# Fused block-sparse attention and gated feed-forward on one core: another TensorE order inside a loop step

## Chip, cores, metric

The kernel runs on one core of one Trainium2 chip. The metric is the device time of one execution in microseconds (us), taken as the median of several runs. Differences are told in us and in per cent of that median.

## What is computed

```python
# attention: 4 batches, 8 heads, 768 positions, 64 per head; blocks of 32
scores = q @ k.T / sqrt(64)                  # kept where the block mask allows
# mask: own block and its neighbours, first and last block row and column,
#       and 3 sampled blocks per block row
attn = softmax(scores);  x = attn @ v        # then tokens x 512
# feed-forward: 3072 tokens, 512 -> 2048 -> 512
h = x @ w_in
out = (h * erf(softplus(h))) @ w_out
```

All of it is done in one launch, from inputs in DRAM to the output in DRAM.

## The kernel before, in words

**Attention units.** Each batch has 15 units, 60 in all: 11 "m" units, each with two block rows and their eight key blocks, and 4 "f" units, which are the dense first and last block rows. A unit passes through `scores` (L619: f32 products on TensorE into `s_m` or `s_f`, one PSUM buffer, `ps_s`, for all units), `soft_max` (L563: the maximum, DVE), `soft_exp` (L572: exponentials `pf` and the high half `p2` in f16, ACT), `soft_low` (L608: the low half on DVE, then a transposing DMA from SP's queue into `pT`). Three unit steps later (`PV_LAG`) follow `values` (L646: `pT` times the gathered values, into `po`), `norm` (L683: the division, DVE, into `xf`, one buffer) and `turn` (L708: a cast on ACT and a subtraction on DVE split `xf` into halves `x2`, and a transposing DMA from SP's queue puts them into `xT`). An m unit gives one such place; of the f units every second one does.

**Feed-forward groups.** Every four places make a chunk, 12 chunks in all; each has 8 groups of 256 hidden columns. A group passes through `ff_first` (L735: 24 matmuls `h<-xT,wi`; three PSUM buffers), `ff_logs` (L759: five activations on ACT), `ff_power` (L772, DVE), `ff_exp` (L777, ACT), and two groups later (`GATE_LAG`) `ff_gate` (L781, DVE, the last reader of `h`) and `ff_halves` (L786, DVE, writes `g`); three groups later (`FF_LAG`) `ff_second` (L794: 12 matmuls `o<-wo,g`), and at a chunk's last group `ff_store` (L807).

**The loop.** L982 runs over 96 groups and three more steps. A step takes one group, and, where the table `spread` says so, one unit and the values of the unit three before: four to seven of a chunk's eight steps have attention work. A step that has both a unit and values is called a full step below; there are 45 of them with a step number of 3 or more, 7 with a unit and no values, 2 with values and no unit. From step 3 on the engines keep the order in which the step is written (`held`, L984); before that, and in the prologue, a scheduler orders the instructions, the loads and the decoding of the weights among them. On TensorE a full step is written: values, first product, scores, second product.

**Values of the next batch.** `behind` (L858) loads, measures and splits the next batch's values in pieces of one unit step each: `load_v` puts the load of `vraw` (one buffer) into SP's queue, and one unit step later `max_v` (L226) reduces it on DVE. SP's queue is in order: each of its DMAs waits for its own data, and all behind it wait too.

```python
if place: values(*place); used_values(place)
if group: ff_first(*group); ff_logs(*group)
if steps: gathers()
if unit:  scores(unit); used_keys(unit)
if m >= FF_LAG: ff_second ...; ff_store ...
```

Of the kernel before, what the change touches and what calls it, by code (L numbers as in the profile page):

```python
# [31 lines left out]
def sparse_attention_moe(ctx: ExitStack, tc: tile.TileContext, qT, kT, v, sampled, w_in, w_out, out):  # L32
# [41 lines left out]
    FF_LAG = 3  # L74
# [488 lines left out]
    def soft_max(unit):  # L563

        s, groups, width = softs[unit]
        tag = "_".join(str(x) for x in unit)
        less = st.tile([P, 4], F32, tag="less", name=f"less_{tag}")[:, :groups]
        dve.tensor_reduce(less, s.rearrange("p (g w) -> p g w", w=width), AX.X, ALU.max, negate=True)
        dve.tensor_scalar(less, less, D**-0.5, None, ALU.mult)
        softs[unit] += (less,)  # L570
# [37 lines left out]
    def soft_low(unit):  # L608

        p2, p3, pf3, n = softs.pop(unit)  # L610
        tag = "_".join(str(x) for x in unit)
        dve.scalar_tensor_tensor(p3[:, :, 1], pf3, P_SCALE, p3[:, :, 0], ALU.mult, ALU.subtract)
        pT = at.tile([P, 16, P], F16, tag="pT", name=f"pT_{tag}", bufs=3)[:, : 2 * n // P]
        sp.dma_start_transpose(out=pT, in_=p2)
        pts[unit] = pT
# [111 lines left out]
    CT = 2  # L727
# [7 lines left out]
    def ff_first(b, ch, fg):  # L735
        tag = f"{b}_{ch}_{fg}"
        if b not in ff_scales:
            isg = st.tile([P, 2], F32, tag="isg", name=f"isg_{b}", bufs=2)
            dve.tensor_scalar(isg, ii, vinv[b], -1.0, ALU.mult, ALU.mult)
            ff_scales[b] = isg  # L740
        part = 2 * fg // NGR
        isg = ff_scales[b][:, part : part + 1]
        h = ps_h.tile([P, W], F32, tag="h", name=f"h_{tag}")
        xT = xTs[b, ch]
        for j in range(FG):
            hj = h[:, j * CW : (j + 1) * CW]
            for kt in range(NK):
                i, c = (fg // 4) * 2 * NK + 2 * kt + fg % 4 // 2, (fg % 2) * CW + j * P
                hi, lo = wi16[:, i, c : c + P], wi16[:, i, 512 + c : 512 + c + P]
                p2_, a = divmod(kt, 2)  # L750
                xa, xb = (xT[:, x * 2 + p2_, :, a * 64 : a * 64 + 64] for x in range(2))
                pe.matmul(hj, hi, xa, start=kt == 0, stop=False)
                pe.matmul(hj, hi, xb, start=False, stop=False)
                pe.matmul(hj, lo, xa, start=False, stop=kt == NK - 1)
        ffs[b, ch, fg] = (h, isg)
# [3 lines left out]
    def ff_logs(b, ch, fg):  # L759

        h, isg = ffs[b, ch, fg]
        tag = f"{b}_{ch}_{fg}"
        x = mo.tile([P, W], F32, tag="x", name=f"x_{tag}")
        act.activation(x, h, AF.Relu, bias=H_CAP, scale=isg)
        act.activation(x, x, AF.Exp, bias=H_CAP, scale=-1.0)
        act.activation(x, x, AF.Ln, bias=1.0, scale=C0)
        y = mo.tile([P, W], F32, tag="s", name=f"y_{tag}", bufs=3)
        act.activation(y, x, AF.Ln, bias=1.0, scale=C1)
        act.activation(x, x, AF.Square, bias=C2)
        ffs[b, ch, fg] = (h, x, y)  # L770
# [10 lines left out]
    def ff_gate(b, ch, fg):  # L781
        h, hs = ffs.pop((b, ch, fg))
        dve.scalar_tensor_tensor(hs, hs, -1.0, h, ALU.add, ALU.mult)
        ffs[b, ch, fg] = hs
# [22 lines left out]
    def ff_store(b, ch, fg, u):  # L807
        t = ch * CT + u
        if fg == NGR - 1:
            o = outs[u]  # L810
            iso = st.tile([P, 1], F32, tag="iso", name=f"iso_{b}_{t}", bufs=2)
            dve.tensor_scalar(iso, unscale, vinv[b], -(2.0**H_SHIFT), ALU.mult, ALU.mult)

            w, n = ((wi, NK * NG), (wo, NF))[u]
            ob = w[:, n, :]
            act.activation(ob, o, AF.Copy, scale=iso)
            r = b * S
            if t < CT * NCH - 1:
                r += (1 + 4 * t) * BLOCK
                act.dma_start(out[r : r + P, :], ob)  # L820
            else:
                act.dma_start(out[r + S - 3 * BLOCK : r + S, :], ob[: 3 * BLOCK])
                act.dma_start(out[r : r + BLOCK, :], ob[3 * BLOCK :])
# [12 lines left out]
    def gathers(most=VGS):  # L836

        nonlocal kfree, vfree
        while kjobs and kfree >= 2 and kjobs[0][0] in have_k:
            kfree -= 2  # L840
            gather(*kjobs.pop(0))
        while vjobs and vfree and most and vjobs[0][0] in have_v:
            gather_v(*vjobs.pop(0))
            vfree -= 1
            most -= 1
# [42 lines left out]
    def used_keys(unit):  # L888
        nonlocal kfree
        if unit[0] == "m":  # L890
            kfree += 2
# [50 lines left out]
    for begun in range(FIRST):  # L942
        with tc.high_priority():
            if begun >= 2:
                place = seen(units[begun - 2])
# [32 lines left out]
        6: (0, 1, 3, 4, 5, 6),  # L978
        7: (0, 1, 3, 4, 5, 6, 7),
    }  # L980
    open_unit = None
    for m in range(len(groups) + FF_LAG):  # L982
        ch, i = divmod(m, NGR)
        held[0] = m >= FF_LAG  # L984
        steps = 0
        if ch < len(until):
            first = until[ch - 1] if ch else FIRST
            steps = int(i in spread[until[ch] - first])
        elif begun < len(units) + PV_LAG:
            steps = 1  # L990
        assert steps in (0, 1)
        group = groups[m] if m < len(groups) else None
        last = groups[m - GATE_LAG] if GATE_LAG <= m < len(groups) + GATE_LAG else None
        unit = unit_of(begun) if steps else None
        old = unit_of(begun - PV_LAG) if steps and begun - PV_LAG >= SEEN else None
        place = seen(old) if old else None
        begun += steps
        if place:
            values(*place)
            used_values(place)  # L1000
        if group:
            ff_first(*group)
            ff_logs(*group)
        if steps:
            gathers()
        if unit:
            scores(unit)
            used_keys(unit)
        if m >= FF_LAG:
            for u in range(CT):  # L1010
                ff_second(*groups[m - FF_LAG], u)
                ff_store(*groups[m - FF_LAG], u)
        if last:
            ff_gate(*last)
        if place:
            norm(*place)
        if last:
            ff_halves(*last)
        low_v()
        if open_unit:  # L1020
            soft_low(open_unit)
        if unit:
            soft_max(unit)
        if place:
            turn(*place)
        if group:
            ff_power(*group)
        if unit:
            soft_exp(unit)
        if group:  # L1030
            ff_exp(*group)
        open_unit = unit
        if unit:
            next_queries(begun - 1)
            behind(begun - 1)
        for n in ((4,), (5,), (6, 7), ())[min(m, FF_LAG)]:
            split_pair(2 * n)

# [34 lines left out]
```

## Time and profile before

| | us |
|---|---|
| median of three runs | 747.17 |
| lowest, highest | 746.92, 754.23 |
| span of the profiled execution, first to last instruction | 742.9 |
| median less span | 4.3 |

| engine | busy us | share of span |
|---|---|---|
| PE (TensorE matmul) | 673.6 | 91% |
| ACT (ScalarE) | 587.1 | 79% |
| DVE (VectorE) | 582.9 | 78% |
| POOL (GpSimd) | 233.3 | 31% |

Of the profiled execution only the span is known; its own device time is taken as the span and the 4.3 us around it. A row of the timeline gives the start of a run of like instructions, its length, engine, line, operation, output and inputs, their number, and in brackets how long the engine was idle before it and what ended that. Nearly all instructions have line 48, that of a recording helper, so they are told apart by their tiles. Matmuls are pipelined, and their ends are modelled; start to start is therefore what is compared. Some 39 us of PE's idle 69 lie in the first 100 us; from 200 us to 700 us it is idle for less than 1 us.

### The profile page before, as it was taken

Reading aid. Unit: us, or ns where it says so; the run is one execution under the profiler, and the core shown is the slowest. Engines: PE = TensorE matmul, PEld = TensorE weight load, DVE = VectorE, ACT = ScalarE, POOL = GpSimd, SP = SyncE. Lnnn points to the kernel's source line nnn. Section 1 sums busy time; section 2 is a strip of 40 time slices with the busy share of each in tenths; the row PEclk is TensorE's granted clock in tenths of the full one; section 3 lists DMA queues with packets and bytes.
Section 4 is the critical chain, followed back from the end, with each engine's and each line's share of the span. In section 5 each row is a group of like instructions: output and inputs, shape, how many; then the busy total and the mean of one; then the engine's idle time right before and its main releaser. Section 6 shows DMA issues by size and latency. Waiting matters only on the chain.

```text
span 742.9 us, 22245 instructions
## 1 busy us (share of the span) xinstructions
PE 673.6 (91%) x9060; PEld 424.2 (57%) x9060; DVE 582.9 (78%) x1151; ACT 587.1 (79%) x1007; POOL 233.3 (31%) x460
## 2 busy tenths in 40 slices
PE   0338775989999999999999999999999999999997
PEld 0123434655666666666666666666666666666663
DVE  5999998879889789787777897986788687655443
ACT  3447789886899978888988888888889788777773
POOL 3348642211755352042543340143444300000000
PEclk9957998999999999999999999999999999999999
DMA  8999643799799999945999899928978665130000
GB/s 308 417 317 295 203 144 71 151 249 186 192 196 223 219 141 224 227 115 130 190 201 200 177 173 233 216 67 174 223 162 202 156 136 139 31 72 9 2 29 28
DMA packets 181030, 126.83 MB, mean 171 GB/s; under 512 B 137664, under 2 KB 154176, under 8 KB 179904
## 3 DMA queue, kind: packets, MB, share of 16 engines
q1 hardware_dynamic: 170688, 98.13, 57.8%
q0 software_dynamic: 5888, 17.84, 9.7%
q10 hardware_dynamic: 4352, 9.44, 4.2%
q8 instruction: 71, 1.16, 0.7%
q14 instruction: 31, 0.25, 0.1%
HBM read 80.45 MB, written 12.95 MB: 126 GB/s over the span
## 4 chain that ended last, share of the span: by engine, by line
PE 75%; DVE 9%; DMA 7%; ACT 7%; issue 1%; SPq 0%; ACTq 0%; DVEq 0%
PE h L48 31%; PE o L48 30%; PE s_m L48 5%; PE po_None L48 4%; DMA wo<-in_w_out_dram 3%; PE s_f L48 3%; ACT x L48 2%; DVE room L48 2%; PE rest L48 2%; DMA wi<-in_w_in_dram 1%; PE po L48 1%; DVE y L48 1%; DMA kr<-in_kT_dram 1%; ACT wo L48 1%; ACT y L48 1%
## 5 line engine op out<-in xcount | busy, mean ns | idle before, releaser
L48 PE MATMUL h<-xT,wi 128*128 128x256 f16 x2304 | 269.6, 274 | 10.8 <-DVE y L48 10.8
L48 PE MATMUL o<-wo,g 128*128 128x512 f16 x1152 | 264.8, 380 | 0.3 <-DVE g L48 0.2
L48 PEld LDWEIGHTS <-wi 128*128 128x128 f16 x2304 | 222.6, 98 | 50.0 <-DVE y L48 7.7
L48 ACT ACTIVATE x<-x 128x512 f32<-128x512 f32 x288 | 181.2, 630 | 8.9
L48 PEld LDWEIGHTS <-g 128*128 128x128 f16 x1152 | 108.2, 98 | 136.7 <-issue 13.3
L48 POOL COPY kbuf<-kx 128x128 f32 (+2 forms) x324 | 121.3, 428 | 87.6 <-PE s_m L48 68.8
L48 POOL DMA_INDIRECT vbuf<-vtab,idx x88 | 92.5, 1051 | 143.5 <-PE po_None L48 83.7
L48 DVE SCALAR_TENSOR_TENSOR y<-y,x 128x512 f32<-128x512 f32 x96 | 67.7, 705 | 84.6 <-ACT x L48 84.6
L48 ACT ACTIVATE y<-y 128x512 f32<-128x512 f32 x96 | 59.6, 621 | 42.7 <-DVE y L48 34.7
L48 ACT ACTIVATE x<-h,isg 128x512 f32<-128x512 f32 x96 | 65.1, 678 | 27.8 <-PE h L48 27.7
L48 ACT ACTIVATE pf_m<-s_m,less_m 128x256 f32<-128x256 f32 x176 | 68.5, 471 | 9.2 <-DVE less_m L48 7.5
L48 DVE SCALAR_TENSOR_TENSOR g<-y,sums,g 128x512 f16<-128x512 f32 x96 | 73.0, 761 | 3.4
L48 DVE SCALAR_TENSOR_TENSOR y<-y,h 128x512 f32<-128x512 f32 x96 | 65.2, 679 | 0.2 <-ACT y L48 0.2
L48 ACT ACTIVATE y<-x 128x512 f32<-128x512 f32 x96 | 60.5, 630 | 2.9
L48 DVE TENSOR_REDUCE less_m<-s_m 128x4 f32<-128x1024 f32 x44 | 53.5, 1217 | 2.5 <-PE s_m L48 2.3
L48 PE MATMUL s_m<-kbuf,qt 64*32 64x256 f32 x1408 | 52.2, 399 | 1.0 <-issue 1.0
L48 DVE TENSOR_SCALAR g<-y,sums 128x512 f16<-128x512 f32 x96 | 48.5, 505 | 1.7
L48 PEld LDWEIGHTS <-pT_m 128*32 128x32 f16 x3168 | 34.3, 97 | 25.0 <-issue 18.9
L48 DVE SCALAR_TENSOR_TENSOR p_m<-pf_m,p_m 128x1024 f16<-128x1024 f32 x38 | 46.3, 1219 | 1.1 <-ACT p_m L48 1.1
L48 PE MATMUL po_None<-vbuf,pT_m 128*32 128x65 f16 (+2 forms) x3168 | 40.7, 204 | 2.4 <-DVE xf L48 1.9
L48 ACT ACTIVATE p_m<-pf_m 128x1024 f16<-128x1024 f32 x38 | 40.2, 1059 | 1.6 <-DMA pT_m<-p_m 0.5
L48 DVE TENSOR_TENSOR x<-xf,x 128x256 f16<-128x256 f32 x44 | 20.0, 454 | 26.4 <-ACT x L48 25.7
(121 smaller groups left out, 558.0 us busy)
## 6 DMA issues: line engine op xcount, KB each, us to landing
vbuf<-vtab SPq DMA_DIRECT2D x80, 195.0 KB, 4.7
vtab<-vn SPq DMA_DIRECT2D x16, 390.0 KB, 5.0
vbuf<-vtab SPq DMA_DIRECT2D x12, 520.0 KB, 5.3
kr<-in_kT_dram SPq DMA_DIRECT2D x16, 384.0 KB, 3.7
vraw<-in_v_dram SPq DMA_DIRECT2D x7, 768.0 KB, 7.5
qt<-in_qT_dram SPq DMA_DIRECT2D x20, 256.0 KB, 4.3
vbuf<-vtab SPq DMA_DIRECT2D x32, 130.0 KB, 6.0
wi<-in_w_in_dram SPq DMA_DIRECT2D x4, 1024.0 KB
```

What stands on the lines that cost most here:

```text
L48: done = call(*args, **kwargs)
```

## The change

A step's order is written anew. On TensorE the scores come ahead of the first product, so that a full step is: values, scores, first product, second product. `ff_power` and `ff_exp` of a group and `turn` of the values come one step later than before; `soft_low` comes one step earlier, at the end of its own unit's step; the logs and the store of the output come behind the softmax.

```diff
         if place:
             values(*place)
             used_values(place)
-        if group:
-            ff_first(*group)
-            ff_logs(*group)
-        if steps:
-            gathers()
         if unit:
             scores(unit)
             used_keys(unit)
+        if group:
+            ff_first(*group)
+        if steps:
+            gathers()
         if m >= FF_LAG:
             for u in range(CT):
                 ff_second(*groups[m - FF_LAG], u)
-                ff_store(*groups[m - FF_LAG], u)
         if last:
             ff_gate(*last)
+        if unit:
+            soft_max(unit)
+        if before:
+            ff_power(*before)
+        if open_place:
+            turn(*open_place)
+        if unit:
+            soft_exp(unit)
+        if before:
+            ff_exp(*before)
+        if group:
+            ff_logs(*group)
+        if m >= FF_LAG:
+            for u in range(CT):
+                ff_store(*groups[m - FF_LAG], u)
         if place:
             norm(*place)
         if last:
             ff_halves(*last)
         low_v()
-        if open_unit:
-            soft_low(open_unit)
-        if unit:
-            soft_max(unit)
-        if place:
-            turn(*place)
-        if group:
-            ff_power(*group)
-        if unit:
-            soft_exp(unit)
-        if group:
-            ff_exp(*group)
-        open_unit = unit
         if unit:
             next_queries(begun - 1)
+            soft_low(unit)
             behind(begun - 1)
+        open_place = place
```

Here `before` is the group of the step before, `open_place` the place whose values were taken in it. Three places show what moves. On PE, in step 16 of the loop (`po` are the value sums, `s_m` the scores, `h` the first product, `o` the second), before the change:

```order
L48 MATMUL h_0_2_0_3650<-xT_0_2_2309,wi_114 128x256
L48 LDWEIGHTS wi_114
L48 MATMUL h_0_2_0_3650<-xT_0_2_2309,wi_114 128x256
L48 MATMUL s_m_1_4_3706<-kbuf1_113,qt_1_2_3386 32x256 x16
L48 LDWEIGHTS g_0_1_5_3554
L48 MATMUL o_0_2_2849<-wo_115,g_0_1_5_3554 128x512
L48 LDWEIGHTS g_0_1_5_3554
```

and with the change, in the same step:

```order
L48 MATMUL po_1_1_None_3593<-vbuf_104,pT_m_1_1_3190 32x65
L48 LDWEIGHTS pT_m_1_1_3190
L48 MATMUL po_1_1_None_3593<-vbuf_104,pT_m_1_1_3190 32x65
L48 MATMUL s_m_1_4_3666<-kbuf1_113,qt_1_2_3400 32x256 x16
L48 LDWEIGHTS wi_114
L48 MATMUL h_0_2_0_3683<-xT_0_2_2362,wi_114 128x256
L48 LDWEIGHTS wi_114
```

The scores stood between the two products and stand now between the value sums and the first product. On DVE, from the same step (`less_m` is the maximum, `x2` the subtraction of the turn, `y` with `x` the power, `y` with `h` the gate, `g` the halves, `p2` the low half), before:

```order
L48 TENSOR_SCALAR g_0_1_6_3743<-y_0_1_6_3297,sums_105 128x512
L48 SCALAR_TENSOR_TENSOR g_0_1_6_3743<-y_0_1_6_3297,sums_105,g_0_1_6_3743 128x512
L48 SCALAR_TENSOR_TENSOR p2_m_1_3_3574<-pf_m_1_3_3569,p2_m_1_3_3574 128x4x256
L48 TENSOR_REDUCE less_m_1_4_3749<-s_m_1_4_3706 128x4
L48 TENSOR_SCALAR less_m_1_4_3749<-less_m_1_4_3749 128x4
L48 TENSOR_TENSOR x2_1_1_3752<-xf_1_1_3739,x2_1_1_3752 128x256
L48 SCALAR_TENSOR_TENSOR y_0_2_0_3679<-y_0_2_0_3679,x_0_2_0_3675 128x512
L48 SCALAR_TENSOR_TENSOR y_0_1_7_3490<-y_0_1_7_3490,h_0_1_7_3461 128x512
```

and now:

```order
L48 TENSOR_REDUCE less_m_1_4_3745<-s_m_1_4_3666 128x4
L48 TENSOR_SCALAR less_m_1_4_3745<-less_m_1_4_3745 128x4
L48 SCALAR_TENSOR_TENSOR y_0_1_7_3577<-y_0_1_7_3577,x_0_1_7_3573 128x512
L48 TENSOR_TENSOR x2_1_0_3750<-xf_1_0_3583,x2_1_0_3750 128x256
L48 SCALAR_TENSOR_TENSOR rinv_1_1_None_3769<-po_1_1_None_3593,level_1_2534 128x4
L48 RECIPROCAL rinv_1_1_None_3769<-rinv_1_1_None_3769 128x4
L48 TENSOR_SCALAR xf_1_1_3772<-po_1_1_None_3593,rinv_1_1_None_3769 128x64
L48 TENSOR_REDUCE xf_1_1_3772<-po_1_1_None_3593 128x192
L48 TENSOR_TENSOR xf_1_1_3772<-xf_1_1_3772,rinv_1_1_None_3769 128x192
L48 TENSOR_SCALAR g_0_1_6_3776<-y_0_1_6_3389,sums_105 128x512
L48 SCALAR_TENSOR_TENSOR g_0_1_6_3776<-y_0_1_6_3389,sums_105,g_0_1_6_3776 128x512
L48 SCALAR_TENSOR_TENSOR p2_m_1_4_3759<-pf_m_1_4_3754,p2_m_1_4_3759 128x4x256
```

The turn and the power behind a unit's maximum are now those of the step before, and the unit's own low half follows in the same step. In SP's queue, at the load of the second half of batch 1's values (`vraw_1_1`, at step 5), before:

```order
L48 DMA vtab_1_107<-vn_1_0_1_1982 128x3x520
L48 DMA_TRANSPOSE pT_m_0_9_2142<-p2_m_0_9_1979 128x16x128
L48 DMA_TRANSPOSE xT_0_1_1518<-x2_0_7_2147 128x4x128
L48 DMA qt_1_0_2160<-in_qT_dram 128x4x128
L48 DMA vraw_1_1_2162<-in_v_dram 128x1536
L48 DMA kr_1_1_2166<-in_kT_dram 128x768
```

and now:

```order
L48 DMA_TRANSPOSE xT_0_1_1583<-x2_0_6_2121 128x4x128
L48 DMA vtab_1_107<-vn_1_0_1_1979 128x3x520
L48 DMA qt_1_0_2154<-in_qT_dram 128x4x128
L48 DMA_TRANSPOSE pT_m_0_10_2157<-p2_m_0_10_2130 128x16x128
L48 DMA vraw_1_1_2159<-in_v_dram 128x1536
L48 DMA kr_1_1_2163<-in_kT_dram 128x768
```

Ahead of the load stood the low half of unit 9 and the turn of place 7; now stand there the turn of place 6 and the low half of unit 10. Multiplicities, shapes and the number of instructions on each engine are the same in both kernels.

## Rows read from the trace of the kernel before

**Rows 1.** 350 to 400 us: busy PE, PEld, DVE, ACT, POOL; granted clock, DMA share, GB/s
```profile
350.00:400.00 50.00, 50.00 (x773) 31.57 (x771) 40.33 (x73) 44.32 (x80) 22.76 (x51) 1.00 1.03 196
```
**Rows 2.** Timeline of PE, one full step (step 15) and the next one's start
```profile
217.41 2.79 PE L48 MATMUL h<-xT,wi 128*128 128x256 f16 x24
220.14 1.09 PE L48 MATMUL s_m<-kbuf,qt 64*32 64x256 f32 x32
221.16 2.76 PE L48 MATMUL o<-wo,g 128*128 128x512 f16 x12
223.86 0.88 PE L48 MATMUL po_None<-vbuf,pT_m 128*32 128x65 f16 x72
224.67 0.50 PE L48 MATMUL h<-xT,wi 128*128 128x256 f16 x3
```
**Rows 3.** Timeline of PE, a step without attention work
```profile
414.81 2.78 PE L48 MATMUL h<-xT,wi 128*128 128x256 f16 x24
417.43 2.75 PE L48 MATMUL o<-wo,g 128*128 128x512 f16 x12
```
**Rows 4.** Timeline of PE, prologue: scores behind values, first product behind scores
```profile
58.03 0.85 PE L48 MATMUL po_None<-vbuf,pT_m 128*32 128x65 f16 x67
58.81 1.07 PE L48 MATMUL s_m<-kbuf,qt 64*32 64x256 f32 x26
...
110.21 1.09 PE L48 MATMUL s_m<-kbuf,qt 64*32 64x256 f32 x30 [0.76 <-issue]
111.23 0.39 PE L48 MATMUL h<-xT,wi 128*128 128x256 f16 x2
```
**Rows 5.** Timeline of PE: first product of step 3; values of the last full step
```profile
128.33 4.85 PE L48 MATMUL h<-xT,wi 128*128 128x256 f16 x24 [7.59 <-DVE y L48]
...
640.08 0.88 PE L48 MATMUL po_None<-vbuf,pT_m 128*32 128x65 f16 x72
```
**Rows 6.** The chain of work that ended last, 158 to 173 us
```profile
159.55 6.45 DMA vraw<-in_v_dram
...
168.42 2.78 PE h L48 x24
```
**Rows 7.** Timeline of PE, step 8: values, dense scores, second product
```profile
164.91 0.88 PE L48 MATMUL po_None<-vbuf,pT_m 128*32 128x65 f16 x72
...
171.13 1.51 PE L48 MATMUL s_f<-kx,qt 64*64 64x512 f32 x8
172.57 0.61 PE L48 MATMUL o<-wo,g 128*128 128x512 f16 x2
```
**Rows 8.** Timelines of SP and of DVE: transposed low half of unit 9; low half of unit 10
```profile
152.60 4.25 SPq L48 DMA_TRANSPOSE pT_m<-p_m  x1
...
157.96 1.22 DVE L48 SCALAR_TENSOR_TENSOR p_m<-pf_m,p_m 128x1024 f16<-128x1024 f32 x1
```
**Rows 9.** Timeline of DVE: maximum, turn, power, then the low half, steps 15 and 16
```profile
221.98 1.22 DVE L48 TENSOR_REDUCE less_m<-s_m 128x4 f32<-128x1024 f32 x1
...
223.92 0.43 DVE L48 TENSOR_TENSOR x<-xf,x 128x256 f16<-128x256 f32 x1 [0.42 <-ACT x L48]
224.26 0.68 DVE L48 SCALAR_TENSOR_TENSOR y<-y,x 128x512 f32<-128x512 f32 x1
...
228.11 1.22 DVE L48 SCALAR_TENSOR_TENSOR p_m<-pf_m,p_m 128x1024 f16<-128x1024 f32 x1
```
**Rows 10.** Busy time in one full step, turn to turn on DVE (columns as rows 1)
```profile
216.66:223.92 7.26, 7.26 (x149) 4.60 (x152) 6.67 (x13) 6.55 (x13) 4.33 (x9) 1.00 1.16 218
```
**Rows 11.** Tile xT: landing of its DMAs; SP and PE at chunks 2 and 11
```profile
DMA to landing us min/median/max: 2.4/4.1/5.8
...
218.56 1.23 SPq L48 DMA_TRANSPOSE xT<-x  x1
...
684.73 1.19 SPq L48 DMA_TRANSPOSE xT<-x  x1
...
688.21 1.04 PE L48 MATMUL h<-xT,wi 128*128 128x256 f16 x8
```

More of the change, by code (lines that the diff above doesn't have):

```diff
@@ L980, in sparse_attention_moe @@
     }
-    open_unit = None
+    open_place = None
     for m in range(len(groups) + FF_LAG):
@@ L997, in sparse_attention_moe @@
         begun += steps
+        before = groups[m - 1] if 1 <= m <= len(groups) else None
         if place:
```

## Prediction

> **What bounds the kernel now.** I read first the busy time of a quiet stretch, then the timeline of TensorE step by step, then the chain of waits, and last the queues that the chain passes through. In the quiet stretch TensorE is busy for all of its 50 us at a granted clock of 1.00, the 2.4 GHz level, while VectorE and ScalarE are busy for 40.33 and 44.32 [rows 1]. A full step takes 7.26 us; in it TensorE is busy for 7.26, VectorE for 6.67, ScalarE for 6.55 [rows 10]. So from some 170 us on the end is set by the sum of what TensorE does, and by nothing else unless another engine becomes later than a step. Before that the chain leaves TensorE: the load of `vraw` (159.55, 6.45 us) holds back a reduction on VectorE, behind which the gate stands that frees `h`, and the first product of step 8 starts at 168.42 [rows 6], which is 8.87 us after the load's issue. TensorE had only the values (164.91) to do meanwhile; the dense scores (171.13) and the second product (172.57) follow [rows 7].
>
> A difference of about 1% of this kernel, 7.5 us, is what can be told from no change. The profiled execution has a span of 742.9 us and 4.3 us around it, 747.2 in all, which is the median; terms are taken off the span, and the 4.3 are left as they are.
>
> **Term 1, TensorE's order in a full step.** No matmul is added or removed, so only what a run of one kind costs because of its neighbours can change. Start to start, in the order of before: values to first product 0.81, first product to scores 2.73, scores to second product 1.02, second product to values 2.70, in all 7.26 [rows 2]. A step without attention work shows the first product directly ahead of the second: 2.62 [rows 3]. Values ahead of scores, and scores ahead of the first product, stand in the prologue: 67 value matmuls take 0.78, which is the rate of 72 in 0.81, and scores take 1.02 ahead of the first product as ahead of the second [rows 4]. The new step is then 0.81 + 1.02 + 2.62 + 2.70 = 7.15, less by 0.11; I use 0.10, as two of the four figures are from fewer matmuls. There are 45 full steps between the wait at 128 us and the last full step at 640 us [rows 5]: 45 x 0.10 = 4.5 us less. In the 7 steps with a unit alone the number of changes between kinds stays the same, and the 2 with values alone are not reordered: nothing. Bounds: 0, if the 0.1 belongs to the scores wherever they stand; -9, if the scores too run 0.1 faster between value sums and first product.
>
> **Term 2, the load that the chain waits for.** In SP's queue the load of `vraw` stood behind the transposed low half of unit 9 (152.60, 4.25 us [rows 8]); now it stands behind that of unit 10, whose low half VectorE made at 157.96 [rows 8]. That would be later, were the low half not a step earlier as well. What ran between turn and low half on VectorE (subtraction, power, gate, five of the division, two of the halves: 223.92 to 228.11, 4.19 us [rows 9]) comes behind it: it starts at 157.96 - 4.19 = 153.8 and ends at 155.0. The transposition held the queue for 4.25 in that row, and one of `xT` for 1.2 [rows 11]; the load then starts between 156.2 and 159.2. I take 157.9, nearer to the row of the same kind. First product of step 8: 157.9 + 8.87 = 166.8. The dense scores (171.13 to 172.57, 1.44 us [rows 7]) now lie ahead of it, in the wait, so the second product starts at 166.8 + 2.62 = 169.4 instead of 172.57: 3.2 us less. Bounds. With the load where it is, 168.42 + 2.62 = 171.0: 1.5 less. With VectorE no earlier than before, the load goes out at 157.96 + 1.22 + 4.25 = 163.4, 3.9 later: 2.4 more. With the load out of the way, TensorE itself is the limit: 164.91, less the scores of step 3 that go into the wait of 7.59 [rows 5] (1.0), less 4 steps of 0.10, plus 0.81 and 1.44, first product at 165.8, 4.2 less in all.
>
> **Term 3, the turn at chunk 2.** `xT` went out at 218.56, some 2.0 us after the values of that step had started, and landed by the median of 4.1 [rows 11] at 222.7; the first product that reads it started at 224.67 [rows 2], so 2.0 were to spare. Now the subtraction of a step's turn runs one step later, behind that step's maximum. With scores ending 1.9 after the values' start, maximum and its small follower take 1.5, the power 0.6, the subtraction 0.4 [rows 9]: the transfer goes out about 4.5 into the step, 2.6 later than before counted from the values that the old turn shared a step with. The first product is 1.0 later too, behind the scores. Of 2.0 + 1.0 to spare 0.4 remain by the median landing; by the longest, 5.8, 1.3 are missing, and the transposition of the unit before may hold SP for 1 us more. I take 0.5, with bounds of 0 and 2.3.
>
> **Term 4, the turn at chunk 11.** Here `xT` went out at 684.73 and the first product started without a wait at 688.21 [rows 11]: the landing took at most 3.5, and I take nothing as spare. No unit is in the step, so the subtraction falls behind one power, 0.6 (224.26 to 224.87 is such a power [rows 9]), of which a part was a wait for ScalarE's cast anyway. I take 0.4, bounds 0 and 0.7. In the other chunks the last turn lies a step or more ahead of its first product, and a step is 7.26 [rows 10], longer than the longest landing: nothing.
>
> **What I cost at nothing.** The scores' one PSUM buffer is read by the exponentials until about 5.0 into the step (1.9 + 1.5 + 1.55), and the next scores come at 7.15 + 0.8: 2.9 us of cover. The second product needs the `g` of the step before, made by about 7 into that step, and comes at 7.15 + 0.81 + 1.02 + 2.62 = 11.6: 4.6 of cover. Power and exponential are a step later, but the gate that needs them is two steps behind its product. Work on VectorE and ScalarE is the same; 6.67 and 6.55 [rows 10] still fit into 7.15, with 0.5 left. If that cover went, each full step would be as long as VectorE's queue.
>
> **Sum.** -4.5 - 3.2 + 0.5 + 0.4 = -6.8: span 736.1, device time 740.4 us.
>
> **Rivals.**
> A, the load gains nothing. Even in the quiet stretch the DMA engines' share is 1.03 [rows 1]; put earlier among other transfers the load may only take longer. Against it: the chain shows what the load waits for, not that it is slow. Only the covered scores remain, 1.5 instead of 3.2: 742.1 us. The Trainium skill, page "Trainium Kernel Development and Optimization", section Key Constraints, says that transfers issued from different engines share the same 16 DMA engines and interleave; by that rule this rival would hold, and the share in the profile agrees that the engines are full.
> B, the order on TensorE saves nothing, since the 0.1 is an entry cost of the attention's small tiles. For it: the 2.62 comes from steps that hold no attention at all. Against it: nothing else differs between 2.73 and 2.62. -3.2 + 0.9: 744.9 us.
> C, both turns are covered and TensorE itself is the limit at step 8. For it: 0.4 to spare by the median landing. -4.5 - 4.2: 738.5 us.
> D, slower: the turn comes a whole step late. It stands on VectorE behind a gate that waits for ScalarE's exponential, which is itself a step later; ScalarE has 0.6 us left in a step. If it runs behind, gate, maximum and subtraction slip, and `xT` goes out a step of 7.26 later: 7.26 - 3.0 = 4.2 at chunk 2, and a step without attention, 5.2 (2.62 twice), at chunk 11, 9.4 in all. With A's 1.5 and term 1: 747.2 - 6.0 + 9.4 = 750.6. After the wait of 7.59 the first product took 4.85 instead of 2.79 [rows 2, 5], which at the lower level of the clock would add 2.1 at either place: 754.8. It decides from new waits of 6.0 us on. Against it: ScalarE's load fits, and the gate's input is not needed until two steps after its product.
>
> **How the numbers follow.** Forecast 0.52, A 0.12, B 0.08, C 0.15, D 0.13. The forecast's own range is 738 to 744. The range for 8 in 10 is 737 to 750: below it is a part of C with a larger term 1, above it most of D. Faster by over 1% means below 739.7: C and a third of the forecast, 0.32. Slower by over 1% means above 754.7: half of D, 0.07. Within 1%: 0.61.
>
> **What would show it.** Term 1: full steps of 7.15 in TensorE's timeline, with 2.62 from first to second product; 7.26 would make it wrong. Term 2: the load issued near 157.9, the dense scores ahead of the first product of step 8, and the second product near 169.4. Terms 3 and 4: an idle of about 0.5 us ahead of the first product at chunks 2 and 11, released by the DMA of `xT`, and nowhere else after 170 us. The forecast as a whole would be wrong if TensorE's idle time after 170 us grew by more than 2 us, or if a wait for `s_m`, `g` or the gate appeared in every full step.

## The result, and the profile after

The changed kernel takes 754.24 us, median of four runs (751.11 to 755.65); the kernel before, beside it, 747.04. The ratio is 1.0112, interval 1.0079 to 1.0145: slower by 1.1%. Forecast was 740.4 with a range of 737 to 750. The sign was wrong.

The profiled execution has a span of 753.9 us and a time of 755.65, so 1.75 us lie around the span, not the 4.3 that I took; by that measure the profiled execution of before (span 742.9) was one of some 744.7 us. The two profiled executions lie 11.0 us apart, the medians 7.2.

Where the 11.0 come from is read off the starts of the first product in steps without a unit, where the moved scores shift nothing: after less before.

| step | 3 | 7 | 10 | 18 | 39 | 42 | 63 | 66 | 87 | 95 |
|---|---|---|---|---|---|---|---|---|---|---|
| us later | 2.78 | 1.53 | 3.48 | 12.13 | 10.75 | 11.29 | 10.82 | 12.05 | 11.32 | 11.62 |

(Step 3 has a unit; its first product comes behind the scores now.) Three places add most of the time: the start, the first step of chunk 1 (step 8), with 2.0 between steps 7 and 10, and the first step of chunk 2 (step 16), with 8.7 between steps 10 and 18. The first steps of chunks 5, 8 and 11 (steps 40, 64 and 88) add 0.5, 1.2 and 0.3. Between such places the changed kernel gains, 1.4 from step 18 to 39.

The gain first. The timeline of TensorE, one full step of the changed kernel (columns as rows 2):

```profile
289.45 2.79 PE L48 MATMUL h<-xT,wi 128*128 128x256 f16 x24
292.08 2.75 PE L48 MATMUL o<-wo,g 128*128 128x512 f16 x12
294.76 0.89 PE L48 MATMUL po_None<-vbuf,pT_m 128*32 128x65 f16 x72
295.58 1.09 PE L48 MATMUL s_m<-kbuf,qt 64*32 64x256 f32 x32
296.61 2.79 PE L48 MATMUL h<-xT,wi 128*128 128x256 f16 x24
```

From first product to first product it is 7.16 instead of the 7.26 of [rows 2, 10]: 2.63 to the second product, 2.68, 0.82, 1.03. That is the forecast step.

The loss stands in the groups of TensorE by tile, from 168 us to the end (busy us, mean ns of one | idle before it and what ended it); of before, then of the changed kernel:

```profile
L48 PE MATMUL h<-xT,wi 128*128 128x256 f16 x2112 | 245.4, 273 | 3.2 <-DVE y L48 3.2
```

```profile
L48 PE MATMUL h<-xT,wi 128*128 128x256 f16 x2112 | 249.6, 276 | 11.1 <-DMA xT<-x 9.6 <-DVE less_m L48 1.4
```

TensorE waits 9.6 us for `xT`, for which it did not wait before, and the same 2112 matmuls take 4.2 us more. Both are at chunk starts. The timeline of TensorE at chunk 1 before the change, where the wait is one for the gate:

```profile
168.42 2.78 PE L48 MATMUL h<-xT,wi 128*128 128x256 f16 x24 [2.63 <-DVE y L48]
```

and at chunks 1 and 2 of the changed kernel, the counterpart of [rows 2, 7]:

```profile
166.45 0.89 PE L48 MATMUL po_None<-vbuf,pT_m 128*32 128x65 f16 x72
167.26 1.51 PE L48 MATMUL s_f<-kx,qt 64*64 64x512 f32 x8
171.88 4.45 PE L48 MATMUL h<-xT,wi 128*128 128x256 f16 x24 [3.11 <-DMA xT<-x]
...
219.75 1.09 PE L48 MATMUL po_None<-vbuf,pT_m 128*32 128x65 f16 x72
220.76 1.09 PE L48 MATMUL s_m<-kbuf,qt 64*32 64x256 f32 x32
221.79 2.79 PE L48 MATMUL h<-xT,wi 128*128 128x256 f16 x24
224.42 2.75 PE L48 MATMUL o<-wo,g 128*128 128x512 f16 x12
227.10 0.89 PE L48 MATMUL po_None<-vbuf,pT_m 128*32 128x65 f16 x72
228.16 1.10 PE L48 MATMUL s_m<-kbuf,qt 64*32 64x256 f32 x32 [0.17 <-DMA qt<-in_qT_dram]
235.19 5.28 PE L48 MATMUL h<-xT,wi 128*128 128x256 f16 x24 [5.93 <-DMA xT<-x]
240.26 3.16 PE L48 MATMUL o<-wo,g 128*128 128x512 f16 x12
```

At chunk 2 it is 5.93 of waiting, 2.5 for a first product of 5.28 instead of 2.79, and 0.4 for the second product: 8.8, the 8.7 of the table. At chunk 5 the wait for `xT` is 0.55. The 1.4 us that are put down to `less_m` stand at chunk 8 and are most likely a wait for `xT` too: the wait of the weight load (PEld) that starts at the same moment is put down to it.

```profile
551.54 2.79 PE L48 MATMUL h<-xT,wi 128*128 128x256 f16 x24 [1.39 <-DVE less_m L48]
551.54 2.52 PEld L48 LDWEIGHTS <-wi 128*128 128x128 f16 x24 [1.87 <-DMA xT<-x]
```

The two slow first products ran at a lower granted clock, 0.50 (the 1.2 GHz level) for the whole of the second; busy time by window (columns as rows 1, the clock is the last figure but two):

```profile
171.88:176.33 4.45, 4.45 (x25) 3.32 (x26) 3.60 (x9) 4.29 (x7) 0.00 (x0) 0.62 1.25 174
235.19:240.47 5.28, 5.28 (x25) 3.63 (x25) 1.00 (x2) 0.00 (x0) 0.00 (x0) 0.50 1.16 296
```

Why `xT` is late is read in SP's queue. Its timeline at chunk 2 (start, time for which the issue held the queue):

```profile
217.34 2.92 SPq L48 DMA_DIRECT2D vbuf<-vtab  x6
220.30 0.43 SPq L48 DMA_DIRECT2D qt<-in_qT_dram  x1
220.83 6.76 SPq L48 DMA_TRANSPOSE pT_m<-p_m  x1
227.69 0.99 SPq L48 DMA_DIRECT2D vbuf<-vtab  x2
228.77 1.19 SPq L48 DMA_TRANSPOSE xT<-x  x1
```

and VectorE's timeline there:

```profile
223.92 0.51 DVE L48 TENSOR_TENSOR x<-xf,x 128x256 f16<-128x256 f32 x1
```

The subtraction was done at 224.43. The transfer went out at 228.77, because the transposition of the low half made at the end of the step before held the queue from 220.83 to 227.59, and two transfers of gathered values (`vbuf`) followed. It landed 6.38 later, at 235.15.

At chunk 1 the same: subtraction done at 160.63, `xT` out at 164.45 behind `pT` (3.16 us), `vraw`, `kr` and `vbuf`, landed after 7.38:

```profile
158.59 3.16 SPq L48 DMA_TRANSPOSE pT_m<-p_m  x1
161.80 0.57 SPq L48 DMA_DIRECT2D vraw<-in_v_dram  x1
162.47 0.90 SPq L48 DMA_DIRECT2D kr<-in_kT_dram  x1
163.47 0.89 SPq L48 DMA_DIRECT2D vbuf<-vtab  x2
164.45 1.19 SPq L48 DMA_TRANSPOSE xT<-x  x1
```

The late start comes out of the same queue. The chain of work behind the first product of step 3 in the changed kernel goes from a transposition in SP's queue through the load of the first half of batch 1's values, its reduction on VectorE (`top_0v`) and the power and gate behind that (start, length):

```profile
115.16 1.45 SPq L48
116.67 9.48 DMA vraw<-in_v_dram
126.18 1.75 DVE top_0v L48
127.94 0.60 DVE y L48
```

TensorE's wait there, the counterpart of [rows 5]:

```profile
131.11 4.79 PE L48 MATMUL h<-xT,wi 128*128 128x256 f16 x24 [11.50 <-DVE y L48]
```

Before the change that load went out 22 us earlier, behind no transposition, and the reduction had no wait:

```profile
94.64 0.36 SPq L48 DMA_DIRECT2D vraw<-in_v_dram  x1
```

### The profile page after: what moved, and what is told of

Read it like the earlier page. It is cut to its first block, busy times and chain, and to the rows that moved or that the text cites. A ratio compares the mean times of both kernels' runs of the same rounds, so it can differ in the third digit from the quotient of the medians.

```text
span 753.9 us, 22228 instructions
## 1 busy us (share of the span) xinstructions
PE 671.7 (89%) x9060; PEld 430.7 (57%) x9060; DVE 576.8 (77%) x1151; ACT 586.6 (78%) x1007; POOL 232.8 (31%) x460
## 4 chain that ended last, share of the span: by engine, by line
PE 76%; DMA 9%; DVE 8%; ACT 3%; issue 2%; SPq 1%; ACTq 0%; DVEq 0%
PE h L48 32%; PE o L48 30%; PE s_m L48 5%; PE po_None L48 4%; PE s_f L48 3%; DMA xT<-x 3%; DVE room L48 2%; DMA wo<-in_w_out_dram 2%; DVE less_m L48 1%; DMA wi<-in_w_in_dram 1%; DMA vraw<-in_v_dram 1%; DVE wo L48 1%; SPq L48 1%; DMA kr<-in_kT_dram 1%; PE po L48 1%
## 5 line engine op out<-in xcount | busy, mean ns | idle before, releaser
L48 PE MATMUL h<-xT,wi 128*128 128x256 f16 x2304 | 274.0, 277 | 23.3 <-DVE y L48 11.5
L48 PEld LDWEIGHTS <-g 128*128 128x128 f16 x1152 | 113.0, 98 | 116.7 <-issue 0.7
L48 POOL COPY kbuf<-kx 128x128 f32 (+2 forms) x324 | 123.8, 429 | 157.6 <-PE s_m L48 141.5
L48 POOL DMA_INDIRECT vbuf<-vtab,idx x88 | 89.4, 1015 | 82.1 <-PE po_None L48 39.6
L48 PE MATMUL rest<-wi,room 128*128 128x512 f32 (+1 forms) x48 | 24.5, 631 | 10.8 <-ACT wi L48 6.5
## 6 DMA issues: line engine op xcount, KB each, us to landing
wi<-in_w_in_dram SPq DMA_DIRECT2D x4, 1024.0 KB, 10.9
```

Of the source, the lines that this page charges most:

```text
L48: done = call(*args, **kwargs)
```

## Experiments

The runs were taken in five groups, in which the kernel before took 745.0 to 754.4 us; a ratio is always to the runs of before in the same group, and kernels are compared in us only within a group. The groups came from several chips; the last two have the same chip number, with before at 753.1 and at 745.2, so the level is not the chip's alone. Theory Q: SP's queue is the cause. Its rivals stand in the expectations.

### One part alone, and parts put back

**The order on TensorE alone** (against the kernel before):

```diff
+        if unit:
+            scores(unit)
+            used_keys(unit)
         if group:
             ff_first(*group)
             ff_logs(*group)
         if steps:
             gathers()
-        if unit:
-            scores(unit)
-            used_keys(unit)
```

> The kernel before, with the scores moved ahead of the first product on TensorE and nothing else moved (SP's queue, VectorE and ScalarE keep the order of before). Theory Q (SP's queue: the changed kernel loses because the transfers of xT and the load of vraw stand behind the transposition of a low half made in the same step; the order on TensorE gains what was forecast): no idle ahead of the first products of chunks 1, 2, 7 and 8, full steps of 7.15 instead of 7.26, about -4.5 for 45 steps and -1.5 at step 8, so 740 to 743 us. Theory P (the order on TensorE is itself the loss, since the first product of a chunk comes 1.03 later and pushes all that hangs on it): no gain or slower, 747 or more.

Measured: 797.66 us, ratio 1.061 (1.052 to 1.071). Neither theory gives the reason, though the time lies in P's open range: there is no wait for `xT`, but a full step takes 9.06 (first products at 230.70 and 239.76) instead of 7.26. The scores wait for their PSUM buffer, since the exponentials of the unit before still stand behind a group's five logs on ScalarE; in step 17 they end at 247.68 and the next scores start at 247.78:

```profile
245.83 0.40 ACT L48 ACTIVATE x<-xf 128x256 f16<-128x256 f32 x1
246.13 1.55 ACT L48 ACTIVATE pf_m<-s_m,less_m 128x256 f32<-128x256 f32 x4
```

So the order on TensorE can't be had without the exponentials ahead of the logs; the parts of the change hang together.

**The turn back in its own step** (against the changed kernel; behind the halves, ahead of the low half):

```diff
-        if open_place:
-            turn(*open_place)
...
         low_v()
+        if place:
+            turn(*place)
```

> The changed kernel, with the turn back in the step of its values, ahead of the unit's low half on VectorE and in SP's queue. Theory Q: xT goes out ahead of the long transposition; the waits of 3.1, 5.9 and 0.5 us ahead of the first products of chunks 1, 2 and 5 go, with the low clock behind the second; the start (first product of step 3 at 131 us instead of 128) stays: 743 to 747 us. Theory P: the waits stay in part, 750 or more.

Measured: 834.83 us, ratio 1.109 (1.100 to 1.118). The waits for `xT` are gone, as Q said, but its time is missed by some 90 us, and P, whose range is open above, expected waits that are not there: the turn's cast now stands behind the logs on ScalarE, and VectorE, which needs it for the subtraction, keeps low half, gate and maximum waiting behind it. Between 250 and 600 us VectorE waited 76.4 us for it, in 22 waits of up to 5.9 us:

```profile
DVE x L48 <- ACT x L48: 76.4, 22, 5.9
```

### The low half later, the loads earlier

**The low half one step later, just behind the turn** (against the changed kernel):

```diff
         if open_place:
             turn(*open_place)
+        if open_unit:
+            soft_low(open_unit)
...
-            soft_low(unit)
             behind(begun - 1)
```

> The changed kernel, with the low half and its transposition one step later, just behind the turn of the step before; the turn keeps its late place. The subtraction of chunk 2 is as late as in the changed kernel (about 4.5 us into the step), only SP's queue differs, and the load of vraw too stands ahead of the transposition. Theory Q: xT goes out right behind its subtraction, some 4 us earlier; the wait at chunk 2 falls from 5.9 to under 2 us, and the start is as before: 741 to 746 us. Theory V (VectorE: the subtraction in the next step is too late whatever the queue does): the waits at chunks 1 and 2 stay above 3 us, 750 us or more.

Measured: 758.83 us, ratio 1.0065 (1.0025 to 1.0105). Q's part about the waits held: none for `xT` is left, which speaks against V, and the first product of step 3 starts at 128.62. Its time did not hold: new pauses stand ahead of the value sums and inside them, 1.41 and 3.32 us ahead of those of steps 5 and 6.

**The loads ahead of the low half**:

```diff
-            soft_low(unit)
             behind(begun - 1)
+            soft_low(unit)
```

> The changed kernel, with the loads of the next batch's values and keys (and their reduction and splitting) ahead of the unit's low half instead of behind it. Theory Q: the load of vraw of the prologue goes out some 20 us earlier and the first product of step 3 starts at 128 instead of 131 us; the second load at 158 instead of 162; the waits of xT stay: 750 to 752 us. Theory S (the start: the late start shifts all later steps against the transfers, and the waits at chunks 1 and 2 follow from it): the waits go as well, 743 to 746 us.

Measured: 760.34 us, ratio 1.0108 (1.0014 to 1.0201), with 9.5 us of waits for `xT`. The loads did go out at 96.1 and 158.9, and the ratio is still that of the changed kernel: the forecast 750 to 752 is missed. The reduction of `vraw` no longer waits, and the wait ahead of the first product of step 3 is 5.34, as in the run with the order on TensorE alone (5.40), not the 11.44 of the run with the turn put back, whose load went out at 116.58. So the load's place makes a wait of 6 us there. What it makes of the start in time these single executions do not settle: the first product stands at 130.87, against 129.77 and 131.40 in those two, and executions of the kernel before alone lie 3.2 us apart there with the same wait of 7.6. The waits for `xT` at chunks 1 and 2 stay all the same, 4.77 and 4.76, which speaks against theory S. At chunk 1 the transposition, which now stands behind the loads, held the queue for 7.14 instead of 3.16, and `xT` went out at 168.45.

### The gathers, and both kernels again

> The kernel before, unchanged, profiled on the chip of these runs, so that waits that belong to a chip are not put down to an edit. The runs of before on the last chip took 754 us instead of 747, and the kernels there showed pauses of 0.5 us inside the value sums. If these belong to that chip, before shows them there too, and not on a chip where it takes 747.

Measured: 746.67 us, ratio 1.001 (0.997 to 1.005), in a group where before takes 745.0. No such pauses; but this execution of before has waits of its own there, 1.48 and 2.88 us for a `pT` at 223 and 234 us.

> The changed kernel, unchanged. A ratio to before of 1.008 to 1.015 again, with waits for xT at chunks 1 and 2 of over 2 us each, if these are the kernel's own and not one execution's.

Measured: 757.05 us, ratio 1.017 (1.011 to 1.023). The first product of chunk 1 waited 3.57 (put down to VectorE's `g`), that of chunk 2 4.42 and that of chunk 8 1.91 for `xT`; at chunk 2 it again went out behind a `pT` that held the queue for 6.88. The loss is the kernel's own.

**The gathers ahead of the scores** (against the changed kernel):

```diff
+        if steps:
+            gathers()
         if unit:
             scores(unit)
...
-        if steps:
-            gathers()
```

> The changed kernel, with the gathers of keys and values put into GpSimd's queue ahead of the scores (as before the change), so that a gather of values does not stand behind a gather of keys that waits for this step's scores. Theory G (GpSimd's queue: gathered values are late in steps 5 and 6, and their transfers share the engines with xT): the pauses ahead of the value sums of steps 5 and 6 go, 2 to 4 us less than the changed kernel. Theory Q (SP's queue alone): same as the changed kernel within 2 us, the waits for xT stay.

Measured: 761.58 us, ratio 1.019 (1.012 to 1.027), with 12.1 us of waits for `xT`. Theory G falls. It is 4.5 us more than the changed kernel, where Q had said within 2; the intervals overlap.

**Both**, gathers ahead and low half behind the turn:

> The low half behind the turn, as in the third run, and the gathers ahead of the scores. Theory Q: no wait for xT; with theory G the pauses of 1.4 and 3.3 us ahead of the value sums of steps 5 and 6 go too, and the kernel beats before by the 4.5 us of the order on TensorE: ratio 0.990 to 0.997. If G is wrong: about the 1.0065 of the third run.

Measured: 746.76 us, ratio 1.0029 (1.0001 to 1.0056). Against the run before it only the low half's place differs, in the queue and on VectorE: 14.8 us less, and 0.4 us of waits for `xT` instead of 12.1. The subtraction at chunk 2 is no earlier for it (4.6 us into its step both times); `xT` goes out 0.6 us behind it instead of 5.5. That is the price of the queue there; a gain over before it is not, since 3.0 us of waiting ahead of the values of step 6 came in.

### The new order from a later step on

Four kernels with the order of before in the first steps, up to step 8 (up to step 3 in the third):

```diff
+        if m < 8:
...
+        else:
```

> The eighth run's order (low half behind the turn, gathers ahead of the scores) from step 8 on, and the order of before in steps 0 to 7. Theory Q+S (in SP's queue the transposition holds xT back; the start is late because the new order of the first steps puts power and exponential a step later where VectorE and ScalarE are the bound): start as before (first product of step 3 at 127 to 128, no pause ahead of the values of step 6), no wait for xT, and the order on TensorE is left as a gain of 0.1 in some 40 full steps: ratio 0.992 to 0.997. If the start is not the first steps' order: about 1.003 again.

Measured: 766.38 us, ratio 1.017 (1.012 to 1.022). Missed: no wait for `xT`, but 9.6 us of pauses at the value sums.

> As the run before it, with the gathers behind the first product as in the changed kernel. If the place of the gathers matters only in the first steps: within 1 us of the run before it; if it delays the values everywhere: 2 us or more above.

Measured: 755.46 us, ratio 1.0019 (0.9988 to 1.0051): 10.9 us less than the run before it, which neither case of the expectation allowed. In this order the gathers belong behind the scores.

> The eighth run's order from step 3 on, the order of before in steps 0 to 2 alone. If the late start is made in the steps that the scheduler orders (0 to 2): like the order from step 8 on, within 1.5 us. If it is made in steps 3 to 7, by the values that wait in step 6: 3 us or more above it.

Measured: 766.29 us, ratio 1.017 (1.012 to 1.022), as from step 8; the gathers cover the question.

> The changed kernel's own order from step 8 on, the order of before in steps 0 to 7. What is left of the loss is that of SP's queue at the later chunks. Theory Q: the wait for xT at chunk 2 of over 4 us stays, with the low clock behind it, and the ratio is 1.003 to 1.010, some 5 to 8 us above the first of these runs. Theory S (all comes from the late start): as the first of these runs.

Measured: 754.25 us, ratio 1.0011 (0.9979 to 1.0044), below what Q expected, and 1.2 us from the run with the low half behind the turn in every step. There the wait for `xT` at chunk 2 is 0, here 3.52; but there the pauses at the value sums are 6.5 us, here 3.8. What the queue gives, a low half that is late in every step takes back. The first product of step 3 is at 127.62 here, and the wait at chunk 2 is there all the same: theory S falls.

### The start, on one chip

> The kernel before, unchanged, beside the three runs that follow on one chip. If pauses of 0.5 us inside the value sums belong to a chip (where before takes 754 us), they are here too whenever they are in the three others; if the change makes them, they are not here.

Measured: 754.74 us, ratio 1.001 (0.996 to 1.005). No pause inside a value sum, while the next three have them (two or three of 0.5 us at step 15 and at step 38). They come with the new order, in the groups where before takes 753 us or more; what TensorE waits for in them the profile does not show, and it stays open.

> The changed kernel, unchanged, on the same chip as the two that follow: 1.008 to 1.018 of before.

Measured: 757.79 us, ratio 1.0066 (1.0019 to 1.0113). A little under what I expected; the waits for `xT` are 2.43 and 3.60.

> The changed kernel's order from step 3 on, the order of before in steps 0 to 2 (which the scheduler arranges among the loads and the decoding). If the start is lost there: first product of step 3 back at 127 to 129 us, and the kernel 3 us or more faster than the changed one. If it is lost in steps 3 to 7 (values and the load of vraw late): within 2 us of the changed kernel.

Measured: 754.78 us, ratio 1.0017 (0.9987 to 1.0048), 3.0 less than the changed kernel. The load of `vraw` goes out at 96.89 again, and the first product of step 3 is at 130.37, between 129.83 (before) and 132.40 (changed).

> The changed kernel's order from step 8 on. On another chip this came to 1.001 of before. If steps 3 to 7 carry the larger part of the loss: 4 us or more faster than the run before it. If steps 0 to 2 carry it: within 2 us of that run. The wait for xT at chunk 2 stays in all three.

Measured: 752.97 us, ratio 0.9985 (0.9945 to 1.0025), 4.8 less than the changed kernel and 1.8 less than the run before it. By the expectation that puts the larger part on steps 0 to 2, where the first load of `vraw` stands; the intervals overlap, so the division is not shown. With the old order up to step 8 the place whose `xT` chunk 1 waits for is turned in its own step, so the wait at chunk 1 goes too; the one at chunk 2 is 6.57.

### `xT` first, only where a chunk closes

The last two take the low half out of its step only where `xT` is waited for: in steps whose values close a chunk.

```diff
+        closes = place and place[2] != 0 and place[1] % CU == CU - 1
...
         if open_place:
             turn(*open_place)
+        if late_unit:
+            soft_low(late_unit)
...
-            soft_low(unit)
+            if not closes:
+                soft_low(unit)
```

In SP's queue this puts one `pT` per chunk behind the `xT` that stood behind it; at chunk 2 it was `pT`, two `vbuf`, `xT` and is now two `vbuf`, `xT`, `pT`.

> The changed kernel, where the low half of a unit is made just behind the turn (instead of in its own step) in those steps alone whose values close a chunk; every other step is as in the changed kernel, the first steps too. Theory Q: at chunk 2 xT goes out right behind its subtraction, 4 us earlier; the waits for xT at chunks 1 and 2 fall below 1.5 us each, the late start stays: 3 to 6 us less than the changed kernel, ratio 1.000 to 1.006. If the time is only handed on to the transposition that now goes out later (values that wait): 1.006 to 1.012.

Measured: 742.40 us, ratio 0.9954 (0.9928 to 0.998). More than expected: 0.5% faster than before, clear of noise, and 1.1 to 2.2% below the three ratios of the changed kernel. SP's queue, the subtraction on VectorE, and TensorE at chunks 1 and 2 in this run:

```profile
217.46 0.78 SPq L48 DMA_DIRECT2D vbuf<-vtab  x2
221.02 1.24 SPq L48 DMA_TRANSPOSE xT<-x  x1
222.36 8.14 SPq L48 DMA_TRANSPOSE pT_m<-p_m  x2
```

```profile
220.49 0.50 DVE L48 TENSOR_TENSOR x<-xf,x 128x256 f16<-128x256 f32 x1
```

```profile
169.33 2.79 PE L48 MATMUL h<-xT,wi 128*128 128x256 f16 x24 [0.49 <-DMA xT<-x]
...
223.67 0.88 PE L48 MATMUL po_None<-vbuf,pT_m 128*32 128x65 f16 x72
224.55 1.11 PE L48 MATMUL s_m<-kbuf,qt 64*32 64x256 f32 x32
225.96 2.78 PE L48 MATMUL h<-xT,wi 128*128 128x256 f16 x24 [0.29 <-DMA xT<-x]
```

The transfer goes out 4.8 us after the values of its step (216.20), not 9.0; the waits are 0.49 and 0.29, and neither first product is slow. The subtraction is as late as in the changed kernel (4.3 to 4.8 us into the step), so theory V falls with this run. At chunk 1 the edit also lets the load of `vraw` out earlier (158.85 instead of 161.80), so what is won there is not the transfer's alone.

> As the run before it, with the order of before in steps 0 to 7. Theory Q: neither the late start nor waits for xT, the 0.1 per full step is left: ratio 0.990 to 0.996, faster than both kernels. If the waits are handed on: 0.997 to 1.003.

Measured: 741.70 us, ratio 0.9952 (0.9923 to 0.998). The first product of step 3 is at 128.60 against 130.86 in the run before it, but by step 13 both stand at 203.2 and 203.4. In this group, with `xT` on time, the late start costs nothing that lasts.

## Why the prediction was wrong

**Term 1 (order on TensorE) was right.** Full steps take 7.15 to 7.16 in every execution of the changed kernel without a wait, 7.26 before. Step by step, that is the 0.1 of the forecast in nearly every full step without a wait. The mended kernel's 0.5% (3.4 us) against before is not this term alone, since the load at chunk 1 is in it too. One reading was loose: 67 value matmuls in 0.78 make 0.84 for 72, not 0.81; 0.82 was measured.

**Term 2 (the load) was wrong.** "I take 157.9": it went out at 161.80, which without the start's 2.8 is 159.0, the late end of my 156.2 to 159.2. The low half started at 156.82, not 153.8, nearly all of that from the late start. But the load no longer decided: the gate ended at 169.79, and the first product waited for `xT` until 171.88. The 3.2 us of gain became a loss of 2.0. Where `xT` is on time (the mended kernel), the second product of step 8 comes 2.2 earlier against the step before it than in the kernel before.

**The start was not in the forecast.** I let the scores of step 3 go into a wait of 7.59 [rows 5] and took the wait's end as fixed. It is 11.50 in the changed kernel. The first product of step 3 stood at 126.63, 128.33 and 129.83 in three executions of before, at 129.50, 131.11 and 132.40 in three of the changed one. It is term 2's own wait, at a load that the term did not look at: the first load of `vraw`, in the prologue, went out at 116.67 instead of 94.64, and the reduction waited 4.35, 4.37 and 4.78 for it in the three executions of the changed kernel, not at all in the three of before. With that load early again (the loads ahead of the low half) that wait was gone. How much of the late start's time is the load's, and how much of the loss is the start's, is not shown.

**Term 3 is the step that failed.** "The transfer goes out about 4.5 into the step": the subtraction was at 4.2 to 4.7 into it, as forecast; the transfer went out at 9.0. I had written that "the transposition of the unit before may hold SP for 1 us more". It held it for 3.2 us more (224.43 to 227.59), two loads for 1.2, and the landing took 6.38 instead of 4.1. The low half, moved a step earlier, was in my text as a help for term 2; that it now stands ahead of every turn in the queue I had read in the order and not priced. In place of 0.5 (bounds 0 and 2.3) chunk 2 cost 8.8: 5.93 of waiting and 2.9 of clock. The hold could have been read in the trace of before: there too the subtraction (216.66 to 217.09) was not what set the transfer's start at 218.56 [rows 11], but a `pT` ahead of it.

```profile
214.34 4.12 SPq L48 DMA_TRANSPOSE pT_m<-p_m  x1
```

**"In the other chunks ... nothing" failed too.** I argued by the distance to the last turn, a step. At chunk 1 that was not enough: from the subtraction to the landing it took 11.2 us (160.63 to 171.83) through the same queue. It cost 3.11 of waiting and 1.7 of clock, 2.0 net, since TensorE had waited 2.63 there for the gate before; the gate alone would now have held the first product until 169.8. At chunk 8 the wait was 1.39, at chunk 5 0.55.

**Term 4 was right**: the first product of chunk 11 starts 0.30 later than a step after the one before (5.51 instead of 5.21), forecast 0.4.

**The rivals.** D had the sign, the price (750.6, with the lower clock 754.8) and the step, a turn that comes 7 us later: `xT` left 9.0 us into the step instead of 2.0. Its place was wrong; VectorE and ScalarE were on time, and the queue behind them was not. That its price fits is luck: it puts 5.2 at chunk 11, where 0.30 was measured, and nothing at the start, at chunk 1 or at chunk 8. Against the mended kernel (0.995 of before) A would be 0.993, the forecast 0.991 and C 0.988, though C's condition, both turns covered, is nearly met there (waits of 0.49 and 0.29 at chunks 1 and 2). Rival A leant on the Trainium skill, page "Trainium Kernel Development and Optimization", section Key Constraints (one set of 16 engines behind all queues). The trace agrees as far as it goes: while `xT` of chunk 2 was under way, from 228.77 to 235.15, the DMA share was 1.29, and its landing took 6.4 us. But the last two runs make the same transfers and change only the place of the low half and its transposition: the order in the queue decides the loss. Of the 10.7 us from the subtraction's end to the landing 4.3 were queue and 6.4 landing. Whether busy engines are also what makes one transposition hold the queue for 7 us and another for 1.5 is open: the hold of 6.76 fell on a DMA share of 1.17 and one of 1.73 (139.98) on 0.31, but one of 1.89 (148.66) on 0.93.

An obvious cure, to put `xT` in ScalarE's queue, was not tried. The Trainium skill, page "DMA: Bandwidth & Descriptors", section "Silent corruption: two transposing streams in flight at once", says that transposing DMAs of two queues in flight together can spoil each other's data; no run here shows it.

## What to carry to other kernels

When an operation with a DMA is moved, write down what stands ahead of each transfer in its queue, with the longest hold that any row shows, before pricing the compute: here the subtraction was forecast to 0.2 us and the transfer missed by 4.5. An edit that moves one transfer earlier for its own sake moves it ahead of others; swap only the pair that matters (one per chunk) rather than the order of every step. And a part of a change may be unable to stand alone: the order on TensorE that gains 0.1 us per step costs 6% without the exponentials moved with it.

## What the runs showed of the hardware

- A transposing DMA of `pT` (128 x 2048 f16, 512 KB by its shape) holds SP's queue for 1.3 to 7.2 us, by the median 3.2, in the changed kernel; a plain load of `vraw` with 768 KB holds it for 0.57 to 1.25. Until the hold ends nothing behind it in that queue goes out. Most of the long holds are near 207, 221, 366, 380, 522 and 536 us, beside runs of six or seven transfers of gathered values (`vbuf`) in the same queue.
- The same first product took 2.78 after a wait of 2.63 (chunk 1 before), 4.45 (granted clock 0.62) after one of 3.11, and 5.28 (0.50, the 1.2 GHz level) after one of 5.93. Behind these two waits the lower clock added half as much again. The length of the wait does not settle it: 4.46 followed one of 1.91 (the changed kernel again, chunk 8), 2.78 one of 2.98 (its order from step 3 on, chunk 2).
- Value sums broke into pieces with pauses of mostly 0.47 to 0.5 us in the new order, in the groups where before took 753 us or more, at steps 15 to 17, 38 and 62. What ends these pauses no view shows.
